# 38 instead of 73 dummy matmuls in TensorE's opening, ahead of the first MLP step

## Chip, cores and metric

The kernel runs on one core of a Trainium2 chip. The metric is the device time of one execution in microseconds (us). Engine names are those of the profile: PE is TensorE, PEld its weight loads, DVE VectorE, ACT ScalarE, POOL GpSimd, SP SyncE, which issues the loads and stores.

## What is computed

A linear-attention recurrence with a decay (4 batches, 8 heads, 768 steps, head dimension 48), whose output goes through a two-layer MLP with an ELU between (384 to 2048 to 384), all in fp32:

```python
for t in range(S):
    cur = np.einsum('bhd,bhe->bhde', u[None] * kt, vt)
    y[:, :, t] = np.einsum('bhd,bhde->bhe', rt, state + cur)
    state = wt[:, :, :, None] * state + np.einsum('bhd,bhe->bhde', kt, vt)
x = y as (B * S, H * D)
h = x @ w_in
g = np.where(h > 0.0, h, np.exp(np.minimum(h, 0.0)) - 1.0)
out = g @ w_out
```

The weights arrive in 64-bit form and are turned into fp32 on the chip.

## The kernel before

The 768 steps are cut into 6 chunks of 128, and each chunk into 4 units (24 in all). A unit's part of the recurrence is done in closed form. The four units of the first chunk go through these steps, which the text names by unit number and the trace by line:

- on DVE two scans of the decay (L436, L446), the product of r and k (L470) and the "hats", which multiply k and r by the scanned decay (L451)
- the *diagonal* on PE (`diag_pe`, L475, needs L470), copied by ACT (L479) and *spread* by ACT over a diagonal matrix (`spread_act`, L485, eight operations)
- the *scores* on PE (`score`, transposes L516 and products L528, needs the hats); ACT copies the transposes out (`trans_out`, L546)
- the *mask* on DVE (`mask`, L540, needs scores and spread)
- the *values* on PE (`value`, L503 and L568, needs mask and L546); ACT copies the result to x (`x_full`, L591)

The diagonal and the transposes share one PSUM bank (`single`, tag "pb"). The scores of units 0, 2 and 3 share two others (`pair`, tag "pa"); unit 1 borrows the accumulators of the MLP (`spare`).

The MLP works on one chunk (512 columns) at a time, in 16 slices of the hidden layer: `g1` (L259 for full fp32 weights, L263 for split ones), ELU on ACT and DVE (L267, L270, L273), `g2` (L291 or L294). In the first chunk six slices use fp32 weights and are done in halves, the first half needing units 0 and 1 alone. Meanwhile the weights are converted: a raw piece is loaded (`load_w`, L606), ACT and DVE work on it (L611, L616 or L618, L626, L630), and its buffer is then free for the next piece.

The order on every engine is fixed when the program is built: `Plan.order` lists all tasks by due times and model durations. Ahead of a task that stands in the table `FILL`, the emitting loop first puts that number of dummy matmuls:

```python
FILL = {("pd", 0): 29, ("s", 0): 12, ("v", 0): 1, ("pd", 1): 5, ("v", 1): 2, ("pd", 2): 7, ("s", 2): 5, ("g1", 0): 12}
...
    def warm(n):
        pw = spare()[2][:, 0:P]
        for _ in range(n):
            nc.tensor.matmul(pw, ones, ones, start=True, stop=True)
...
        for t in plan.order():
            warm(FILL.get(t["key"], 0))
            t["fn"]()
```

("pd", i) is the diagonal of unit i, ("s", i) its scores, ("v", i) its values and ("g1", 0) the first MLP product. A fill multiplies a 128x128 tile of ones by itself into an accumulator bank that the MLP clears later; nobody reads its result, and it waits for nothing but the ones. It stands in PE's queue, so what is behind it waits until it is done.

Of the kernel before, what the change touches and what calls it, by code (L numbers as in the profile page):

```python
# [41 lines left out]
LOW = ['DVE']*2+['ACT']*14  # L42
RAWS = ["raw0", "raw1", "x1a", "x1b"] * 2 + ["raw0", "raw1"] * 4
DUE = {0: 9.0}
FILL = {("pd", 0): 29, ("s", 0): 12, ("v", 0): 1, ("pd", 1): 5, ("v", 1): 2, ("pd", 2): 7, ("s", 2): 5, ("g1", 0): 12}


def _pieces():
    res = []
    for h in range(H):  # L50
        s, e = h * D, (h + 1) * D
        while s < e:
# [36 lines left out]
             g1={16: -3.5, 19: -3.5, 20: 4.25, 23: 5.75, 29: -7.5, 30: -8.25, 31: -13.25, 33: 21, 38: -15.75, 40: -29.75, 42: -33.75, 44: -17.5, 48: -70.75, 51: 26.75, 55: 44, 56: -10.5, 58: -10, 68: 34, 82: -8, 83: 12.5, 84: 6, 93: -7.5},  # L89
# [4 lines left out]
             s={4: -29.75, 9: -2.25, 12: -30.25, 13: 5, 21: 8.5},  # L94
             sp={4: -19.25, 5: 8.75, 9: 39.5, 13: 29.5, 17: -6.5},
             v={2: -5.5, 15: -2, 17: 6.75, 18: 24, 20: 22.25})
# [225 lines left out]
def rwkv_elu_kernel(ctx, tc, wkr, rk, vp, u, uz, gkrw, gv, gu, wraw, out):  # L322
# [84 lines left out]
# [4 lines that stand above are left out]
# [424 lines left out]
    with tc.manual_schedule():  # L835
# [3 lines that stand above are left out]
# [137 lines left out]
```

## Time and profile before

| | us |
|---|---|
| median of 3 runs | 518.42 (518.3 to 519.65) |
| the profiled execution | 517.97 |
| its span in the trace | 515.8 |
| PE busy in the span | 506.8 (98%) |
| PEld busy | 417.8 (81%) |
| DVE busy | 335.4 (65%) |
| ACT busy | 270.6 (52%) |
| mean granted clock | 0.997 |

The span is the stretch from the first to the last instruction of the program; the rest of the execution's time, 2.2 us, lies around it. Busy shares are means over stages with different limits. A matmul's duration in the trace overlaps the next one's, so the pace is read from one start to the next, not from durations.

### The profile page before, as it was taken

To read this page: it belongs to the slowest core of one execution; us is meant where nothing else is said; L and a number is where in the kernel's file an instruction comes from. 1 tells how busy PE (TensorE), PEld (TensorE's weight loads), DVE (VectorE), ACT (ScalarE), POOL (GpSimd) and SP (SyncE) were. 2 spreads that over 40 slices of the span, in tenths; PEclk is the share of its full clock that TensorE was granted. 3 is DMA by queue.
4 is the path that set the end of the run, shared out by engine and by line. 5 is a ranking of instruction groups with operands and counts; after the bars stand their busy time and mean duration, and the time that the engine had idled before them with its cause. 6 is when DMAs were issued, how large, how long until landed. Compare 5 with 4: busy or idle time off the path is not lost.

```text
span 515.8 us, 13882 instructions
## 1 busy us (share of the span) xinstructions
PE 506.8 (98%) x6070; PEld 417.8 (81%) x6070; DVE 335.4 (65%) x469; ACT 270.6 (52%) x520; POOL 97.1 (19%) x94
## 2 busy tenths in 40 slices
PE   9999999999999999999999999999999999999995
PEld 9998787787888888888788888887888877888884
DVE  6789999999589643498743487842499642423242
ACT  2779667657655344565545564443545443535351
POOL 2000123103455100264100174400161100000000
PEclk9999999999999999999999999999999999999998
DMA  8936944600843000856200674202332000010001
GB/s 258 337 132 201 319 139 142 189 3 4 260 117 106 3 3 3 243 154 160 57 19 3 197 204 143 75 0 79 99 101 56 22 1 3 0 62 0 1 1 66
DMA packets 18882, 51.09 MB, mean 99 GB/s; under 512 B 2304, under 2 KB 2688, under 8 KB 18816
## 3 DMA queue, kind: packets, MB, share of 16 engines
q1 hardware_dynamic: 18672, 50.08, 32.0%
q8 instruction: 49, 0.80, 0.6%
q14 instruction: 17, 0.14, 0.1%
q10 hardware_dynamic: 144, 0.07, 0.0%
HBM read 45.42 MB, written 4.72 MB: 97 GB/s over the span
## 4 chain that ended last, share of the span: by engine, by line
PE 86%; DVE 5%; ACT 3%; DMA 2%; issue 2%; POOL 0%; DVEq 0%; ACTq 0%; SPq 0%; POOLq 0%
PE ph L263 33%; PE acc L294 33%; PE pa L503 6%; PE acc L410 4%; PE pa L528 3%; PE pa L568 2%; PE ph L259 2%; PE acc L291 2%; PE pb L516 1%; DMA wx<-in_wkr_dram 1%; DMA wraw<-in_wraw_dram 1%; DVE m L273 1%; ACT m L270 1%; DVE wg L626 1%; ACT wg L611 1%
## 5 line engine op out<-in xcount | busy, mean ns | idle before, releaser
L273 DVE SCALAR_TENSOR_TENSOR m<-m,ph 128x512 f32<-128x512 f32 (+1 forms) x102 | 66.3, 651 | 98.3 <-ACT m L270 98.0
L267 ACT ACTIVATE m<-ph 128x512 f32<-128x512 f32 (+1 forms) x102 | 58.2, 571 | 108.7 <-PE ph L263 97.0
L263 PE MATMUL ph<-xh,w_l 128*128 128x512 f32 x270 | 105.4, 390 | 0.0
L294 PE MATMUL acc<-gh,w_l 128*128 128x512 f32 x268 | 104.6, 390 | 0.0
L281 DVE TENSOR_TENSOR gl<-m,gh 128x512 fp32r<-128x512 f32 x90 | 65.2, 726 | 39.4 <-ACT gh L277 39.3
L277 ACT CAST gh<-m 128x512 fp32r<-128x512 f32 x90 | 55.7, 619 | 59.4 <-PE acc L294 30.5
L294 PE MATMUL acc<-gh,w_h 128*128 128x512 f32 x180 | 71.9, 399 | 0.0
L263 PE MATMUL ph<-xh,w_h 128*128 128x512 f32 x180 | 71.6, 398 | 0.1
L294 PE MATMUL acc<-gl,w_h 128*128 128x512 f32 x180 | 70.3, 390 | 0.0
L263 PE MATMUL ph<-xl,w_h 128*128 128x512 f32 x180 | 70.1, 390 | 0.0
L270 ACT ACTIVATE m<-m 128x512 f32<-128x512 f32 (+1 forms) x102 | 61.9, 607 | 2.2
L263 PEld LDWEIGHTS ph<-xh,w_l 128*128 128x128 f32 x270 | 50.7, 188 | 10.9
L294 PEld LDWEIGHTS acc<-gh,w_l 128*128 128x128 f32 x268 | 50.3, 188 | 10.7
L458 POOL TENSOR_TENSOR rk<-rk 128x384 f32<-128x384 f32 x20 | 28.3, 1416 | 121.2 <-DMA rk<-in_rk_dram 116.7
L496 POOL TENSOR_SCALAR_AFFINE_SELECT am<-md 64x512 f32<-64x512 f32 x32 | 29.1, 910 | 113.5 <-DVE md L465 56.3
L263 PEld LDWEIGHTS ph<-xh,w_h 128*128 128x128 f32 x180 | 33.8, 188 | 7.8 <-DVE m L273 0.5
L294 PEld LDWEIGHTS acc<-gh,w_h 128*128 128x128 f32 x180 | 33.8, 188 | 7.7
L294 PEld LDWEIGHTS acc<-gl,w_h 128*128 128x128 f32 x180 | 33.8, 188 | 6.8 <-DVE gl L281 0.2
L263 PEld LDWEIGHTS ph<-xl,w_h 128*128 128x128 f32 x180 | 33.8, 188 | 6.7
L263 PE MATMUL ph<-xh,w_g 128*128 128x512 f32 x90 | 36.3, 403 | 0.1
L263 PE MATMUL ph<-xl,w_g 128*128 128x512 f32 x90 | 35.1, 390 | 0.0
L294 PE MATMUL acc<-gh,w_g 128*128 128x512 f32 x88 | 34.8, 396 | 0.0
(116 smaller groups left out, 754.2 us busy)
## 6 DMA issues: line engine op xcount, KB each, us to landing
wraw<-in_wraw_dram SPq DMA_DIRECT2D x16, 768.0 KB, 5.4
k<-in_wkr_dram SPq DMA_DIRECT2D x24, 448.0 KB, 6.7
rk<-in_rk_dram SPq DMA_DIRECT2D x20, 384.0 KB, 4.2
v<-in_vp_dram SPq DMA_DIRECT2D x24, 256.0 KB, 6.8
w<-in_wkr_dram SPq DMA_DIRECT2D x24, 227.9 KB, 4.4
out_dram<-o SPq DMA_DIRECT2D x17, 256.0 KB, 2.1
wx<-in_wkr_dram SPq DMA_DIRECT2D x8, 227.9 KB, 2.9
ub<-in_u_dram SPq DMA_DIRECT2D x1, 192.0 KB, 4.5
```

The source lines that it names most:

```text
L263: nc.tensor.matmul(ph, w[f][:, 0, k], y[:, k], start=(k == n == 0), stop=(k == NK - 1 and n == 2))
L267: act(s["m"], s["ph"], AF.Relu, scale=-1.0)
L270: act(s["m"], s["m"], AF.Exp, scale=-1.0)
L273: stt_(s["m"], s["m"], -1.0, s["ph"], ALU.add, ALU.max)
L277: nc.scalar.copy(s["gh"], s["m"])
L281: nc.vector.tensor_tensor(s["gl"], s["m"], s["gh"].bitcast(F32), ALU.subtract)
L294: nc.tensor.matmul(a_, w[f][:, 1, m], fold(s, g[:, a:b]), start=(first and n == 0), stop=(final and n == 2))
L410: nc.tensor.matmul(pw, ones, ones, start=True, stop=True)
L458: eng.tensor_tensor(u_["rk"][:, 0], u_["rk"][:, 0], u_["rk"][:, 1], ALU.mult)
L496: nc.gpsimd.affine_select(out=am[rs].rearrange("t q p s -> t (q p) s"), in_=u_["md"][rs].rearrange("t q p -> t (q p)").unsqueeze(2).broadc ...
L503: nc.tensor.matmul(u_["py"][32 * j:32 * j + 32, h, k], l, r, **flags)
L528: nc.tensor.matmul(pa[1 - q][ts, p], u_["k"][rs, p, ts], u_["r"][rs, p, ts], start=True, stop=True)
```

## The change

One table of numbers: fewer fills ahead of seven of the eight tasks.

```diff
-FILL = {("pd", 0): 29, ("s", 0): 12, ("v", 0): 1, ("pd", 1): 5, ("v", 1): 2, ("pd", 2): 7, ("s", 2): 5, ("g1", 0): 12}
+FILL = {("pd", 0): 15, ("s", 0): 6, ("v", 0): 1, ("pd", 1): 4, ("v", 1): 1, ("pd", 2): 3, ("s", 2): 2, ("g1", 0): 6}
```

The order on DVE, POOL and SP is the same as before. On ACT a few rows differ in the general path, which runs only if the decays are out of range and doesn't run with these inputs. On PE the start of the program now stands like this (L410 are the fills, L475 the diagonals, L516 and L528 the scores):

```order
 L970 UNCONDITIONAL_BRANCH
-L410 MATMUL acc<-ones 128x128 x29
+L410 MATMUL acc<-ones 128x128 x15
 L475 MATMUL pb<-ubd,rkc 128x2 x4
-L410 MATMUL acc<-ones 128x128 x12
+L410 MATMUL acc<-ones 128x128 x6
 L516 MATMUL pb<-ident,k 128x112 x4
 L528 MATMUL pa<-k 128x128 x8
-L410 MATMUL acc<-ones 128x128 x5
+L410 MATMUL acc<-ones 128x128 x4
 L475 MATMUL pb<-ubd,rkc 128x2 x4
```

Only counts differ; 14 fills fewer stand ahead of unit 0's diagonal, 6 ahead of its scores, 1 ahead of unit 1's diagonal. On PE around the first MLP product (L259) and unit 2's scores, behind unit 1's values (L568):

```order
 L568 MATMUL acc<-v,kt 64x48
 L568 MATMUL acc<-v,kt 48x48
-L410 MATMUL acc<-ones 128x128 x12
+L410 MATMUL acc<-ones 128x128 x6
 L259 MATMUL ph<-xf,w_f 128x256 x6
-L410 MATMUL acc<-ones 128x128 x5
+L410 MATMUL acc<-ones 128x128 x2
 L516 MATMUL pb<-ident,k 128x112 x4
 L528 MATMUL pa<-k 128x128 x8
```

Six fills fewer stand ahead of the first MLP product and three ahead of unit 2's scores. Between the two places, unit 2's diagonal has 4 fewer ahead of it and unit 1's values 1 fewer.

## Rows read from the trace of the kernel before

**Rows 1.** Busy time by stretch: length, each engine's busy us (instructions), granted clock, DMA.

```profile
40.00:60.00 20.00, 19.47 (x140) 15.89 (x140) 19.42 (x27) 17.74 (x36) 3.62 (x4) 1.00 0.80 254
101.00:200.00 99.00, 98.53 (x1635) 80.16 (x1636) 73.69 (x103) 53.02 (x97) 25.86 (x22) 1.00 0.22 65
```

**Rows 2.** Timeline of PE, 0 to 37 us: start us, length us, engine, line, operation.

```profile
1.07 9.63 PE L410 MATMUL acc<-ones 128*128 128x128 f32 x58 [1.07 <-POOL ones L377]
10.54 0.95 PE L475 MATMUL pb<-ubd,rkc 112*128 112x2 f32 x8
11.35 2.92 PE L410 MATMUL acc<-ones 128*128 128x128 f32 x24
14.11 0.55 PE L516 MATMUL pb<-ident,k 112*128 112x112 f32 x4
...
15.68 1.38 PE L410 MATMUL acc<-ones 128*128 128x128 f32 x10
16.90 0.95 PE L475 MATMUL pb<-ubd,rkc 112*128 112x2 f32 x8
17.71 0.47 PE L410 MATMUL acc<-ones 128*128 128x128 f32 x2
...
21.34 1.83 PE L410 MATMUL acc<-ones 128*128 128x128 f32 x14
23.01 0.95 PE L475 MATMUL pb<-ubd,rkc 112*128 112x2 f32 x8
...
26.05 2.94 PE L410 MATMUL acc<-ones 128*128 128x128 f32 x24
28.83 2.75 PE L259 MATMUL ph<-xf,w_f 128*128 128x256 f32 x12
31.42 1.28 PE L410 MATMUL acc<-ones 128*128 128x128 f32 x10
32.53 0.55 PE L516 MATMUL pb<-ident,k 112*128 112x112 f32 x4
...
36.39 0.86 PE L503 MATMUL pa<-am,v 128*32 128x128 f32 x24
```

**Rows 3.** Busy time in single microseconds: the first number in brackets counts PE's passes.

```profile
6.00:7.00 1.00, 1.00 (x7) 1.00 (x7) 1.00 (x3) 0.00 (x0) 0.00 (x0) 1.00 1.02 406
8.00:9.00 1.00, 1.00 (x12) 1.00 (x11) 1.00 (x2) 0.00 (x0) 0.00 (x0) 1.00 1.04 262
30.00:31.00 1.00, 1.00 (x7) 0.87 (x6) 0.74 (x1) 0.67 (x2) 0.00 (x0) 1.00 0.00 0
```

**Rows 4.** Timeline of DVE, 0 to 37 us; in square brackets idle time before, and releaser.

```profile
8.06 1.20 DVE L451 TENSOR_TENSOR k<-k,eg 112x1024 f32<-112x1024 f32 x1
...
15.90 1.35 DVE L540 COPY_PREDICATED am<-upper,pa 128x512 f32<-128x512 uint32 x2 [4.68 <-PE pa L528]
...
28.64 0.96 DVE L626 SCALAR_TENSOR_TENSOR w_f<-w_f,wraw 128x768 uint32<-128x768 uint32 x1 [0.91 <-ACT wraw L616]
29.52 1.22 DVE L451 TENSOR_TENSOR k<-k,eg 112x1024 f32<-112x1024 f32 x1
31.86 0.42 DVE L273 SCALAR_TENSOR_TENSOR m<-m,ph 128x256 f32<-128x256 f32 x1 [1.12 <-ACT m L270]
32.65 0.96 DVE L626 SCALAR_TENSOR_TENSOR w_f<-w_f,wraw 128x768 uint32<-128x768 uint32 x1 [0.37 <-ACT wraw L616]
...
35.00 1.33 DVE L540 COPY_PREDICATED am<-upper,pa 128x512 f32<-128x512 uint32 x2
```

**Rows 5.** Timeline of ACT, 0 to 37 us.

```profile
11.79 2.45 ACT L485 ACTIVATE am<-ident,md 128x128 f32<-128x128 f32 x8
...
14.93 0.51 ACT L546 COPY kt<-pb 128x448 f32<-128x448 f32 x1
...
26.55 0.46 ACT L591 COPY xf<-acc 128x384 f32<-128x384 f32 x1
```

**Rows 6.** The chain of work that ended last, 80 to 100 us, its longest piece.

```profile
86.74 6.19 DMA wraw<-in_wraw_dram
```

## Prediction

> **What bounds the kernel now.** I read the busy time by stage first, then TensorE's timeline of the first 37 us, then what VectorE and ScalarE wait for there. From 101 to 200 us TensorE is busy 98.53 of 99 us, VectorE 73.69 [rows 1]: nothing on PE is left to squeeze there, and work that begins earlier ends earlier. From 40 to 60 us PE is busy 19.47 of 20 us and VectorE 19.42 [rows 1]: both are full, so a gain of the opening reaches the end only if both engines get it.
>
> In the opening PE has no idle time after 1.07 us [rows 2]. It is full because fills stand between the real steps, and the question is whether a step starts when its inputs are ready or when the fill ahead of it is done. An fp32 fill matmul shows as two passes, so the 29 fills are the x58 at 1.07 us [rows 2]. The other engines answer the question: VectorE sits idle 4.68 us and then waits for PE's scores (L528), not PE for VectorE [rows 4]. Unit 0's hats end on VectorE at 8.06 + 1.20 = 9.26 us [rows 4], and its scores, which need them, begin on PE at 14.11 [rows 2]. The fills hold the real work back there.
>
> **What a fill costs.** The block of 24 passes at 26.05 lasts until 28.83, the one of 14 at 21.34 until 23.01 [rows 2]: 2.78 less 1.67 is 1.11 us for 10 passes, 0.112 us a pass. The first block is slower. If its last 28 passes took 0.112 each, its first 30 took 10.54 - 3.13 - 1.07 = 6.34 us, 0.211 each. The counts say the same: 7 passes touch the microsecond 6 to 7, 12 the one from 8 to 9 [rows 3]. So PE ran at its lower level (1.2 GHz) for some 6 us after its first matmul and at 2.4 GHz after that. The column PEclk shows 1.00 in both [rows 3]; I believe the pace of the passes.
>
> **The change, part by part.** It takes out 35 matmuls, 70 passes, all of them at 0.112 us if the clock rises where it does now: 28 passes ahead of unit 0's diagonal (3.13 us), 12 ahead of its scores (1.34), 2 ahead of unit 1's diagonal (0.22), 8 ahead of unit 2's diagonal (0.89), 2 ahead of unit 1's values (0.22), 12 ahead of the first MLP product (1.34), 6 ahead of unit 2's scores (0.67). Sum: 7.81 us. Each block is gained only as far as the step behind it has its inputs:
>
> - Unit 0's diagonal moves from 10.54 to 7.41. Its product (L470) is written before the second scan and the hats of 8.06 [rows 4], so it is ready by then. Gain 3.13.
> - Unit 0's scores move from 14.11 to 9.64. The hats end at 9.26. ScalarE's spread of unit 0 (11.79, 2.45 long) [rows 5] follows the diagonal and moves by 3.13, to 8.66 to 11.11. The mask (15.90 on VectorE) waits for scores and spread; the scores now end last, and the mask moves by 3.13 + 1.34 = 4.47, to 11.43. VectorE's idle time of 4.68 shrinks to 0.2.
> - Unit 1's diagonal would move to 12.21. It reuses unit 0's score bank, which ScalarE's copy (14.93, 0.51 long) [rows 5] must have left. That copy stands behind the spread and a weight conversion of some 0.8 us, so it now ends at about 12.3. PE waits 0.2 us.
> - The first MLP product moves from 28.83 by 6.95, to about 21.9. It needs unit 1's x (26.55 + 0.46 = 27.01) [rows 5], which hangs on unit 2's diagonal and moves by 3.13 + 1.34 + 0.22 - 0.2 + 0.89 = 5.4, to 21.6. It is just in time.
> - Unit 2's scores would move from 32.53 to 24.9. They need unit 2's hats on VectorE (29.52 + 1.22 = 30.74) [rows 4]. VectorE had moved by 4.46 at the first mask and gains the 0.91 it sat idle ahead of L626, since ScalarE is earlier too; so the hats end at 25.4 and PE waits 0.5.
> - Unit 2's values (36.39) need the mask at 35.00 on VectorE, 1.33 long. VectorE also loses the idle 1.12 and 0.37 [rows 4]: 4.46 + 0.91 + 1.12 + 0.37 = 6.86. The mask ends at 29.5, and PE waits 0.3 more.
>
> So PE gains 7.81 less waits of 0.2 + 0.5 + 0.3, that is 6.8, and VectorE gains 6.86 by its own idle time. Both engines carry the same 6.8 us into the full stage that follows, and I take **6.8**. What else could stand still is the loads. The first six pieces of raw weights leave in a full queue that runs dry by 30 us (0 GB/s from 30 to 31) [rows 3]. The fifth is converted on ScalarE between the spreads of units 2 and 3; if it has to wait for its landing it starts at most near 28, against 27 by the shift, and nothing before 33 us needs it. I cost that at nothing. From there each load is issued when a buffer comes free, so it moves along.
>
> The profiled execution took 517.97 us, 2.2 more than its span; less 6.8 that is 511.2. It lies 0.45 under the median of the runs (518.42), so my forecast for the median is **511.6 us**.
>
> Bounds of the sum: with no new wait at all it is 7.81 us, 510.6, or 510.1 on the profiled execution's level; with VectorE getting no more than its first 4.46, 514.0.
>
> **The rivals.**
>
> *The clock is lost (slower).* The fills also keep PE working, and the first 30 passes show what PE costs at the lower level: 0.211 against 0.112, 0.9 us more for each us of work. If with half the fills PE ran at 1.2 GHz from 7.41 until the first MLP product at 21.9, 14.5 us of work would take 13 us more: 524.6. It decides from 7.5 us of work at the lower level on, where 6.8 us is eaten up. Against it: PE's new idle time is 1 us in all. And from 16.90 to 21.34 the kernel before has just 2 passes of fill among diagonal, values and scores, yet the 14 passes that follow run at 0.112 [rows 2]: the level held through such a stretch, and the change makes more of them. Chance 0.09. The Trainium skill has a rule that speaks for this rival (TensorE: Matmul & The Clock Gate, section The HAM clock gate): the throttled state is the default, sustained matmul activity releases it and idleness brings it back. By that rule alone the thinner opening risks the 524.6; the trace agrees with it at the start, where the passes took 0.211, and shows no fall in the thin stretch.
>
> *The clock rises later.* The 30 passes that stay end at 7.41, and the rise comes shortly before that. In an execution where it comes only during unit 0's scores, the 3.9 us from 7.41 to 11.3 take up to 3.5 us more, and all that follows is late by as much: 511.6 to 515.1. For it: the fill now ends close to the rise. Against: PE goes straight on with diagonal, 12 passes and scores. Chance 0.11.
>
> *VectorE keeps its small waits.* If the idle 0.91, 1.12 and 0.37 stay, because ScalarE's chain of spread and conversion is no earlier than the first 4.46 us, VectorE brings just that into the full stage: 514.0. It was busy 19.42 of 20 us from 40 to 60 [rows 1], so it can't catch up. Against: ScalarE's operations there hang on PE steps that move by 5.4 and more. Chance 0.08. The Trainium skill (Perfetto Trace Analysis, section Identifying the Most-Contended Engine) warns that TensorE's matmul busy share is no measure of headroom and that weight-load time is. From 40 to 60 us weight loads are busy 15.89 of 20 [rows 1], so by that rule VectorE is the fuller engine and this case would be the one to bet on.
>
> *The gain is swallowed.* The chain of waits holds 6.19 us of waiting for a raw weight load from 86.74 on [rows 6]. If that load came at a fixed time, the opening would not matter: 518.4. Against: it is issued when a conversion frees its buffer, which moves too. Chance 0.05.
>
> **How the numbers follow.** Forecast 0.67; clock later 0.11, VectorE's waits 0.08, swallowed 0.05, clock lost 0.09. A measurement of this kernel tells about 0.3% (1.6 us) from no change; all of the first three lie beyond that on the fast side. So faster 0.86, same 0.05, slower 0.09. The range runs from 510.1 (no new wait) to 514.8, which takes in VectorE's case and most of the late clock.
>
> **What would show it.** In the new profile the first block of fills should end near 7.4 us and the first mask start near 11.4, with hardly any idle time before it; the first MLP product should start near 21.9, unit 2's mask near 28.2; PE's waits in the opening should sum to about 1 us; and every stage after 40 us should look as before, 6.8 us earlier. I am wrong if passes after 8 us take over 0.2 us, if VectorE still waits before L626 or L273 in the opening, or if the stage from 50 to 101 us gets longer.

## The result and the profile after

The changed kernel takes **512.17 us** (median of 4 runs, 511.97 to 512.88) against 518.36 for the kernel before beside it (4 runs, 517.35 to 519.65): a ratio of 0.9882 (the changed kernel's time over that of the kernel before), 95% interval 0.9858 to 0.9906. The forecast was 511.6. The execution profiled took 512.88 us, its span is 510.8.

TensorE's timeline of the opening in the changed kernel (start us, length us, engine, line, operation; in square brackets idle time before and its releaser):

```profile
1.07 5.55 PE L410 MATMUL acc<-ones 128*128 128x128 f32 x30 [1.07 <-POOL ones L377]
7.05 1.05 PE L475 MATMUL pb<-ubd,rkc 112*128 112x2 f32 x8 [0.43 <-DVE rkc L470]
7.97 1.59 PE L410 MATMUL acc<-ones 128*128 128x128 f32 x12
9.55 0.57 PE L516 MATMUL pb<-ident,k 112*128 112x112 f32 x4
...
12.14 1.02 PE L475 MATMUL pb<-ubd,rkc 112*128 112x2 f32 x8
...
21.68 2.76 PE L259 MATMUL ph<-xf,w_f 128*128 128x256 f32 x12
...
25.26 0.58 PE L516 MATMUL pb<-ident,k 112*128 112x112 f32 x4 [0.38 <-PE acc L410]
...
29.40 1.08 PE L503 MATMUL pa<-am,v 128*32 128x128 f32 x32 [0.19 <-DVE am L540]
```

Against [rows 2], unit 0's diagonal begins at 7.05 instead of 10.54, its scores at 9.55 instead of 14.11, the first MLP product at 21.68 instead of 28.83, unit 2's values at 29.40 instead of 36.39. PE now waits three times, 0.43, 0.38 and 0.19 us, 1.0 in all. The first block of fills ended some 0.8 us sooner than forecast, because the clock rose sooner (the same 30 passes lasted 5.55 us here and 6.45 in the run again below), and PE then waited for the product L470; the gain there stopped at what VectorE allows.

VectorE's timeline, same kernel:

```profile
8.06 1.20 DVE L451 TENSOR_TENSOR k<-k,eg 112x1024 f32<-112x1024 f32 x1
...
11.36 1.35 DVE L540 COPY_PREDICATED am<-upper,pa 128x512 f32<-128x512 uint32 x2 [0.16 <-PE pa L528]
...
23.07 0.95 DVE L626 SCALAR_TENSOR_TENSOR w_f<-w_f,wraw 128x768 uint32<-128x768 uint32 x1
...
25.08 0.41 DVE L273 SCALAR_TENSOR_TENSOR m<-m,ph 128x256 f32<-128x256 f32 x1
25.67 0.96 DVE L626 SCALAR_TENSOR_TENSOR w_f<-w_f,wraw 128x768 uint32<-128x768 uint32 x1 [0.18 <-ACT wraw L616]
...
28.01 1.33 DVE L540 COPY_PREDICATED am<-upper,pa 128x512 f32<-128x512 uint32 x2
```

The hats still begin at 8.06; the idle 4.68 before the first mask is 0.16, and the 0.91, 1.12 and 0.37 of [rows 4] are 0, 0 and 0.18. Unit 2's mask begins at 28.01 instead of 35.00. So VectorE carries 6.99 us into the full stage, PE as much (36.39 to 29.40). ScalarE shows the one load that stands still in the opening:

```profile
20.97 0.46 ACT L591 COPY xf<-acc 128x384 f32<-128x384 f32 x1
...
27.58 0.92 ACT L611 ACTIVATE w_f<-wraw 128x768 f32<-128x768 f32 x1 [0.66 <-DMA wraw<-in_wraw_dram]
```

It waits 0.66 for the fifth raw piece, and nobody waits for it. The stages behind the opening, by stretch (length, busy us of each engine, granted clock, DMA):

```profile
40.00:60.00 20.00, 18.30 (x114) 15.41 (x106) 18.25 (x24) 13.09 (x29) 2.66 (x2) 1.00 0.93 287
101.00:200.00 99.00, 99.00 (x1519) 80.38 (x1518) 71.23 (x98) 50.95 (x93) 25.23 (x22) 1.00 0.22 65
```

The steady stage is as full as in [rows 1]. The microseconds 40 to 60 now hold work that stood at 47 to 67. There 1.2 us of the gain go, as PE's timeline shows, first in the change, then in the kernel before:

```profile
49.66 1.56 PE L291 MATMUL acc<-m,w_f 128*128 128x256 f32 x6 [0.55 <-DVE m L273]
...
53.67 1.56 PE L259 MATMUL ph<-xf,w_f 128*128 128x256 f32 x6 [1.15 <-DVE m L273]
```

```profile
56.28 1.56 PE L291 MATMUL acc<-m,w_f 128*128 128x256 f32 x6 [0.19 <-DVE m L273]
...
59.48 1.56 PE L259 MATMUL ph<-xf,w_f 128*128 128x256 f32 x6 [0.34 <-DVE m L273]
```

PE waits for VectorE 0.36 us longer at the first place and 0.81 longer at the second: of the 6.99 us, 6.62 are left at the first (49.66 against 56.28) and 5.81 at the second (53.67 against 59.48). Behind the first loss stands a load. ScalarE's and VectorE's timelines in the change:

```profile
41.78 0.94 ACT L616 ACTIVATE wraw<-wraw 128x768 uint32<-128x768 uint32 x1 [0.68 <-DMA wraw<-in_wraw_dram]
```

```profile
43.84 0.56 DVE L588 TENSOR_TENSOR xl<-xf,xh 128x384 fp32r<-128x384 f32 x1 [0.47 <-ACT xh L584]
```

ScalarE waits for the ninth raw piece, and VectorE then for ScalarE; the kernel before has neither wait. The piece is issued 7.0 us earlier than before (35.9 against 42.9) but takes 5.8 us to land instead of 4.3. Behind the second loss stands a scan. VectorE's timeline, 50 to 60 us, and GpSimd's, 40 to 60 us:

```profile
51.26 2.04 DVE L436 TENSOR_TENSOR_SCAN eg<-w,reset 112x520 f32<-112x520 f32 x1
...
58.36 1.23 DVE L436 TENSOR_TENSOR_SCAN eg<-w,reset 112x520 f32<-112x520 f32 x1
```

```profile
50.96 1.25 POOL L458 TENSOR_TENSOR rk<-rk 128x384 f32<-128x384 f32 x1 [3.37 <-DMA rk<-in_rk_dram]
```

The same scan and product in the kernel before:

```profile
57.89 1.23 DVE L436 TENSOR_TENSOR_SCAN eg<-w,reset 112x520 f32<-112x520 f32 x1
```

```profile
58.36 1.54 POOL L458 TENSOR_TENSOR rk<-rk 128x384 f32<-128x384 f32 x1 [4.15 <-DMA rk<-in_rk_dram]
```

The scan of unit 5 starts 6.63 us earlier (51.26 against 57.89) and ends 5.82 earlier (53.30 against 59.12): it takes 2.04 instead of 1.23. Before, it began first and GpSimd's product was the stretched one (1.54; 1.00 us where nothing is beside it); now the product's data (unit 5's r and k) land in time for it to begin first. PE's second wait is for the operation right behind this scan (L273), so it loses the 0.81 us with VectorE. VectorE gets 0.42 of it back, since in the kernel before the subtraction L645 that follows is stretched in its turn (1.37 us; 0.95 in the change), but PE has lost its time by then.

What is left stays to the end. The chain of waits of the change, 80 to 110 us:

```profile
82.41 7.76 DMA wraw<-in_wraw_dram
...
94.86 0.65 DVE am L542
95.50 0.04 issue
95.55 1.17 PE pa L503 x71
```

It goes through another raw piece than the chain of [rows 6]. Two pieces are issued one after the other there; SyncE's timeline, first of the change, then of the kernel before:

```profile
80.93 1.81 SPq L606 DMA_DIRECT2D wraw<-in_wraw_dram  x2
```

```profile
86.74 1.81 SPq L606 DMA_DIRECT2D wraw<-in_wraw_dram  x2
```

Both are issued 5.81 us earlier and take about as long as before (6.2 and 7.8 us; 6.2 and 7.9 before), so these loads moved along. The values after them (101.47 before, 95.55 now) come 5.92 earlier. The last store is issued at 504.18 instead of 510.13, 5.95 earlier:

```profile
504.18 0.38 ACTq L309 DMA_DIRECT2D out_dram<-o  x1
```

From there to the end of the span are 6.6 us in this execution, 5.7 in that of before; the other three runs' spans are 509.9 to 510.3.

### The profile page after: what moved, and what is told of

Read it like the earlier page. It is cut to its first block, busy times and chain, and to the rows that moved or that the text cites. A ratio compares the mean times of both kernels' runs of the same rounds, so it can differ in the third digit from the quotient of the medians.

```text
span 510.8 us, 13742 instructions
## 1 busy us (share of the span) xinstructions
PE 498.9 (98%) x6000; PEld 409.6 (80%) x6000; DVE 336.5 (66%) x469; ACT 270.7 (53%) x520; POOL 94.8 (19%) x94
## 4 chain that ended last, share of the span: by engine, by line
PE 84%; DVE 5%; ACT 5%; DMA 3%; issue 1%; DVEq 0%; SPq 0%; ACTq 0%
PE acc L294 35%; PE ph L263 34%; PE pa L503 6%; DMA wraw<-in_wraw_dram 3%; PE pa L528 2%; PE pa L568 2%; PE pb L516 1%; PE ph L259 1%; ACT wraw L616 1%; PE acc L291 1%; DVE wg L626 1%; ACT m L270 1%; PE acc L410 1%; DVE m L273 1%; ACT m L267 1%
## 5 line engine op out<-in xcount | busy, mean ns | idle before, releaser
L273 DVE SCALAR_TENSOR_TENSOR m<-m,ph 128x512 f32<-128x512 f32 (+1 forms) x102 | 66.3, 651 | 96.6 <-ACT m L270 96.4
L458 POOL TENSOR_TENSOR rk<-rk 128x384 f32<-128x384 f32 x20 | 26.4, 1321 | 120.6 <-DMA rk<-in_rk_dram 120.2
```

The costliest lines, as they stand in the source:

```text
L273: stt_(s["m"], s["m"], -1.0, s["ph"], ALU.add, ALU.max)
L458: eng.tensor_tensor(u_["rk"][:, 0], u_["rk"][:, 0], u_["rk"][:, 1], ALU.mult)
```

## The experiments

My theory was that of the prediction: each block of fills is gained for itself, the gains add up, and both engines carry them on. Rivals: the fills' worth is the clock they hold; the gain of a part alone is lost on the way; and, once the profile after was seen, that the 0.8 us of the scan is a race between a load and VectorE. Each group of runs has runs of the kernel before beside it on the same chip ("before" in the brackets below); the chips differ from group to group.

### The two halves of the change

first15 takes out only the 14 fills ahead of unit 0's diagonal; rest_only takes out all the others and leaves that block. In the cuts here and below, a line with a plus alone stands in the place of the kernel's line `FILL`.

```diff
-FILL = {("pd", 0): 29, ("s", 0): 12, ("v", 0): 1, ("pd", 1): 5, ("v", 1): 2, ("pd", 2): 7, ("s", 2): 5, ("g1", 0): 12}
+FILL = {("pd", 0): 15, ("s", 0): 12, ("v", 0): 1, ("pd", 1): 5, ("v", 1): 2, ("pd", 2): 7, ("s", 2): 5, ("g1", 0): 12}
```

> Only the first block goes from 29 to 15 fills, all others as before. Theory (a fill is dead time up to the point where an input binds): unit 0's diagonal about 3.1 us earlier, VectorE's wait before the first mask 4.68 - 3.1 = 1.6 us, all behind moves by 3.1; end at 518.4 - 3.1 = 515.3 (514.8 to 515.8). Rival, gain comes from the later blocks alone: 518.4. Rival, gain is not additive because VectorE's later idle time is what counts: under 1 us.

```diff
+FILL = {("pd", 0): 29, ("s", 0): 6, ("v", 0): 1, ("pd", 1): 4, ("v", 1): 1, ("pd", 2): 3, ("s", 2): 2, ("g1", 0): 6}
```

> The first block stays at 29 fills, all others as in the change. Theory: VectorE gains 1.34 at the first mask and its idle 0.91 + 1.12 + 0.37 later, 3.7 in all; PE's 4.69 less waits of about 1 us gives the same; end at 518.4 - 3.7 = 514.7 (514.2 to 515.4). With the run that changes the first block alone this should add up to the change's gain, 6.2 to 6.8. Rival, only the first block matters: 518.4.

Measured: first15 517.07 (12 runs; before 517.46, 35 runs), ratio 1.0, 0.9972 to 1.0029; rest_only 515.25 (12 runs), 0.9956, 0.993 to 0.9981. Their openings do what the sum says: unit 2's mask begins at 31.67 and at 31.25, 3.33 and 3.75 earlier than before, together 7.08 where the whole change has 6.99. But by the last store (508.64 and 510.12 against 510.13) 1.49 and nothing is left. The execution of rest_only that was profiled took 518.3 us, 3 us more than the median of its runs; by medians 2.2 us of its gain arrive, and 515.25 lies within the times expected (which start from 518.4, not from 517.46), while first15 misses its 515.3. First the waits of VectorE, 36 to 110 us (waiting and releasing line: us in total, times, longest), of first15, then of rest_only:

```profile
DVE wg L626 <- ACT wg L611: 2.3, 1, 2.3
```

```profile
DVE wg L626 <- ACT wg L611: 2.1, 1, 2.1
```

This is behind a raw weight piece, the tenth, that took 6.2 us (first15) and 5.9 (rest_only) from issue to landing, where before, and in the change, it took 4.3 and 4.2. Second, collisions as in the change, here with the subtraction L645. VectorE's timeline in first15:

```profile
52.09 0.97 DVE L626 SCALAR_TENSOR_TENSOR wg<-wg,wraw 128x768 uint32<-128x768 uint32 x1 [2.31 <-ACT wg L611]
52.97 1.76 DVE L645 TENSOR_TENSOR w_l<-wg,w_h 128x768 fp32r<-128x768 f32 x1
...
58.19 1.75 DVE L645 TENSOR_TENSOR w_l<-wg,w_h 128x768 fp32r<-128x768 f32 x1
```

GpSimd's product began at 52.55 and at 58.13, just ahead of both. And in rest_only the clock falls behind PE's wait. PE's timeline, then the busy times by stretch (PE, PEld, DVE, ACT, POOL, then the granted clock):

```profile
54.42 2.77 PE L291 MATMUL acc<-m,w_f 128*128 128x256 f32 x6 [2.08 <-DVE m L273]
```

```profile
53.00:54.00 1.00, 0.00 (x0) 0.00 (x0) 1.00 (x2) 0.00 (x0) 0.22 (x1) 1.00 1.07 294
...
55.00:58.00 3.00, 3.00 (x9) 2.37 (x8) 3.00 (x5) 1.61 (x4) 0.58 (x1) 0.50 0.87 239
```

In first15 PE was idle from 53 to 55 us too, and the clock stayed at 1.00. The fall seems to come in some executions only: the three longest of rest_only's 12 runs, the profiled one among them, have a mean granted clock of 0.991 to 0.993, the other nine 0.996 to 0.998.

So an opening gain of 3.3 or 3.8 us isn't yet a gain of the kernel: in these two profiles most of it goes in the stage from 40 to 60 us, behind a load that lands late. "The gain is swallowed" is right for first15 and in part for rest_only, in a way I had not thought of. By medians the halves give 0.4 and 2.2 us, the whole 6: they don't add up. That the same load is behind it in the executions without a profile is not shown.

### Is the long raw piece the doing of the code's length?

In first15 a 16 KB packet of the instruction queue fell into the long piece. first15_pad has first15's fills and 14 tiny matmuls, so that PE's code is as long as before:

```diff
             warm(FILL.get(t["key"], 0))
+            for _ in range(14 * (t["key"] == ("pd", 0))):
+                nc.tensor.matmul(spare()[2][0:32, 0:32], ones[:, 0:32], ones[:, 0:32], start=True, stop=True)
             t["fn"]()
```

> As the run with 15 fills in the first block and all others as before, plus 14 dummy matmuls of 32 columns ahead of unit 0's diagonal, so that PE's code is as long as in the kernel before; they cost PE under 1.5 us. Theory (with the shorter code a 16 KB code fetch falls into the tenth raw weight piece, which then takes 6.2 us instead of 4.3): the piece takes about 4.3 us again, VectorE's wait of 2.3 us before L626 near 52 us is gone, end 2 to 3 us under the kernel before. Rival (that piece is slow for another reason, or at random): end as without the padding, level with the kernel before or up to 1 us above.

Measured: 517.29 (12 runs; before 518.55), ratio 0.9966, 0.9941 to 0.9991. The tenth piece took 4.6 us and VectorE waited 0.7 instead of 2.3 us. But the end stayed where it was (last store at 508.79, 1.34 earlier than before), since GpSimd's product now got ahead of L626 (1.73) and of a scan (2.04). The piece and its wait went as the code fetch would have it; the time didn't, and only_first and no_fill below, whose code is shorter still, show 4.2 us for that piece. Nor is such a packet enough to make a piece long: in all six profiles with the change's fills one follows the issue of the ninth piece within 0.6 us, and that piece took 4.2, 4.3, 4.4 and 4.5 us in four of them (swap_loads, late_load, again_b, again), 5.6 and 5.8 in two (swap_b, the change). **Not settled.**

### What the remaining fills are for

only_first keeps nothing but 15 fills ahead of unit 0's diagonal, no_fill nothing at all.

```diff
+FILL = {("pd", 0): 15}
```

> 15 fills ahead of unit 0's diagonal, none anywhere else. Theory (the remaining later fills stand in idle time): PE's waits take the place of the fills, the first mask at most 0.3 us earlier, end within 0.5 us of the change's 512.2. Rival (clock): with PE idle a third of the time from 7 to 25 us the clock falls, passes take 0.21 us again, 0.9 us for each us of work: 514 to 522.

```diff
+FILL = {}
```

> No fill at all, so PE's first work is unit 0's diagonal near 7.05 us. Rival (clock): PE begins at the lower level; if it rises during unit 0's scores, the first mask is 1 to 1.5 us later than with the change, 513.5; if it rises only with the first MLP product, 516 to 520. Theory that fills do nothing for the clock: 512.2, as with the change.

Measured: only_first 514.87, ratio 0.9939 (0.9911 to 0.9966); no_fill 514.75, 0.9929 (0.9901 to 0.9958); 12 runs each, before 517.46. Both beat the kernel before and neither reaches the change (0.9866 and 0.9872 in its two other measurements). For only_first the rival came true, not the theory; no_fill lies between the cases named. The busy times by stretch of only_first show why:

```profile
6.00:9.00 3.00, 2.00 (x17) 1.78 (x16) 3.00 (x4) 0.96 (x5) 0.00 (x0) 1.00 1.03 317
9.00:12.00 3.00, 2.58 (x20) 2.33 (x20) 2.17 (x4) 2.96 (x8) 0.00 (x0) 0.56 1.03 276
...
20.00:26.00 6.00, 5.78 (x61) 4.92 (x60) 5.78 (x8) 4.10 (x12) 0.00 (x0) 0.50 1.04 308
26.00:27.00 1.00, 1.00 (x5) 0.86 (x4) 0.79 (x2) 0.86 (x2) 0.00 (x0) 0.78 1.01 418
```

The clock had risen; PE then sat idle 1.41 us before unit 0's scores, the clock fell to the lower level (0.50 is 1.2 of 2.4 GHz), and it came back between 26 and 27 us. All 12 runs of only_first have a mean granted clock of 0.978 to 0.988, all 16 of the change one of 0.995 to 0.998. PE's timeline, only_first and then no_fill:

```profile
9.42 0.98 PE L516 MATMUL pb<-ident,k 112*128 112x112 f32 x4 [1.41 <-DVE reset L445]
...
12.34 1.87 PE L475 MATMUL pb<-ubd,rkc 112*128 112x2 f32 x8
...
24.93 3.59 PE L259 MATMUL ph<-xf,w_f 128*128 128x256 f32 x12 [0.22 <-ACT xf L591]
```

```profile
7.12 1.87 PE L475 MATMUL pb<-ubd,rkc 112*128 112x2 f32 x8 [7.12 <-DVE rkc L470]
...
25.58 3.54 PE L259 MATMUL ph<-xf,w_f 128*128 128x256 f32 x12 [0.21 <-ACT xf L591]
```

A diagonal of 0.95 takes 1.87 in both. The fills that the change leaves hold the clock, and that is worth 3.9 us at unit 2's mask (31.95 in only_first, 28.01 in the change) and 2.4 to 3.6 us at the end: the medians, from different chips, are 514.87 and 512.43 (the change in 12 runs), and against the kernel before beside each only_first gains 2.6 us, the change 6.0 and 6.2. The Trainium skill (TensorE: Matmul & The Clock Gate, section The HAM clock gate) has idleness bring the throttled state back; the trace agrees in only_first, where the clock fell behind 1.41 us of it, and shows that it need not: in first15 the clock stayed through 2.35 us.

### The first block longer instead of shorter

```diff
+FILL = {("pd", 0): 43, ("s", 0): 12, ("v", 0): 1, ("pd", 1): 5, ("v", 1): 2, ("pd", 2): 7, ("s", 2): 5, ("g1", 0): 12}
```

> The kernel before with 14 fills more in the first block, 43 in place of 29. Theory (dead time, 0.112 us a pass): unit 0's diagonal at 10.54 + 3.13 = 13.67, all behind it 3.1 us later, end 3.1 us over the kernel before (518.0 to 518.5 so far), that is near 521.3. Rival (the stage from 40 to 61 us takes up part of a shift of the opening, as it did when the first block alone was shortened): 0 to 2 us over it.

Measured: 520.59 (12 runs; before 518.72), ratio 1.0027, 1.0004 to 1.005: 1.9 us slower by medians, and at most 2.6. The diagonal of unit 0 begins at 13.24 instead of 10.54 and unit 2's mask at 37.70 instead of 35.00, both 2.70 later for 14 fills, not 3.1: the clock rose earlier in this execution than in that of before. It ends 3.62 later there (last store at 513.75; this execution took 1.4 us more than the median), with a scan of 2.03 us in the way. Between the two theories: a first block costs what it takes in the opening, and the stage after adds or takes away a microsecond.

### Which load lands first

again is the change once more; swap_loads has unit 5's r and k load issued after its load of w, so that GpSimd's product comes later.

> The change as it is, once more, beside the two runs below on one chip. Theory: the opening is 6.8 to 7 us earlier in every execution, and what scatters lies behind 50 us (raw weight loads of 4.2 or 6 us, a scan beside GpSimd); so about 6 us under the kernel before, with the scatter of the kernel before (some 4 us). Rival (clock): the clock falls in some executions because the fills are thin; then some runs lie 2 us and more above the rest and show a lower mean granted clock (under 0.994).

```diff
-        for t in plan.order():
+        tasks = plan.order()
+        place = {t["key"]: n for n, t in enumerate(tasks)}
+        one, two = place["ld_rk", 5], place["ld_w", 5]
+        tasks[one], tasks[two] = tasks[two], tasks[one]
+        for t in tasks:
```

> The change, with unit 5's r-and-k load issued after unit 5's decay load instead of before it. Theory (the 0.8 us lost near 51 us is GpSimd's product, started by that load, blocking VectorE's scan): the product starts later, the scan (L436) near 51.3 us takes 1.23 us instead of 2.04, PE behind it stays 6.6 us early instead of 5.8, end 0.8 us below the change. Rival (the loss comes from the loads' lengths): the scan's duration changes, the end does not.

Measured: again 512.58 (6 runs; before 518.55), ratio 0.9872, 0.9839 to 0.9905; swap_loads 510.97 (6 runs), 0.9848, 0.9815 to 0.9882. This time the change itself had no blocked scan (none stretched by the product). VectorE's and GpSimd's timelines in again:

```profile
50.89 1.23 DVE L436 TENSOR_TENSOR_SCAN eg<-w,reset 112x520 f32<-112x520 f32 x1
```

```profile
51.52 1.39 POOL L458 TENSOR_TENSOR rk<-rk 128x384 f32<-128x384 f32 x1 [4.31 <-DMA rk<-in_rk_dram]
```

The product began 0.63 after the scan, and the last store was issued at 503.36, 6.77 earlier than before. So the same program keeps or loses the 0.8 us from one execution to the next. I repeated both, and put the swap on the kernel before.

> The change a third time, as the measure for the two runs below. Opening as in its two profiles (first MLP product near 21.7 us, PE's idle time 1 us). Whether VectorE's scan near 51 us takes 1.23 or 2.04 us is open in one execution: theory says that it is 2.04 when unit 5's r-and-k load lands before the scan starts, 1.23 when it lands after. End 512 to 513.

> The exchanged loads a second time. Theory (GpSimd's product blocks the scan in some executions of the change and in none of this one): scan 1.23 us, PE at 61 us about 7 us earlier than in the kernel before, end 0.4 to 1.6 us under the change on the same chip. Rival (the first comparison was scatter): level with the change within 0.3 us.

> The kernel before, all 73 fills, with the same two loads exchanged. In its profile the scan started 0.5 us ahead of GpSimd's product and was not blocked, so theory expects little: 0 to 0.8 us under the kernel before, by the executions in which it is blocked. Rival (the exchange helps for another reason, such as an earlier decay load): 1 to 2 us under it, as in the change.

Measured (before 518.36, 17 runs): again_b 512.14 (6 runs), 0.9866 (0.9828 to 0.9904); swap_b 511.67 (6 runs), 0.9859 (0.9822 to 0.9896); before_swap 517.88 (12 runs), 1.0001 (0.9975 to 1.0028). In both again_b and swap_b the scan was blocked (2.04 us), in swap_b against what was expected; their last stores are at 505.27 and 504.40. PE's wait right behind the scan tells the two cases apart: 1.15 or 1.16 us in every profile in which the product began first (the change, again_b, swap_b, first43, first15_pad), 0.34 in before, again, swap_loads and late_load, in which the scan did. Swapping two neighbours doesn't decide the race, and without the change it is worth nothing. late_load therefore issues unit 5's r and k after its w and its k:

```diff
+        tasks = plan.order()
+        late = next(t for t in tasks if t["key"] == ("ld_rk", 5))
+        tasks.remove(late)
+        tasks.insert(next(n for n, t in enumerate(tasks) if t["key"] == ("ld_k", 5)) + 1, late)
+        for t in tasks:
```

> The change, with unit 5's r-and-k load issued after unit 5's decay load and its k load (the exchange put it after the decay load alone, and in its second profile the product still started 0.08 us ahead of the scan). Theory: the product can't start before 52.5 us, the scan near 51 us takes 1.23 us in every execution, PE at 61 us 6.8 to 7.3 us earlier than in the kernel before, end 511.0 to 511.5. Rival (the product then blocks the next operation of VectorE, a 0.95 us subtraction, by as much): scan 1.23, subtraction 1.7, end as with the change, 512 to 512.6.

Measured: 511.46 (6 runs, 510.51 to 512.69; before 518.72), ratio 0.985, 0.9818 to 0.9882. VectorE's and GpSimd's timelines:

```profile
51.12 1.22 DVE L436 TENSOR_TENSOR_SCAN eg<-w,reset 112x520 f32<-112x520 f32 x1
...
55.34 1.81 DVE L446 TENSOR_TENSOR_SCAN eg<-w,reset 112x520 f32<-112x520 f32 x1
```

```profile
54.13 1.92 POOL L458 TENSOR_TENSOR rk<-rk 128x384 f32<-128x384 f32 x1 [6.71 <-DMA rk<-in_rk_dram]
```

The first scan is free, the product now meets the second (1.81 instead of 1.24). The last store is issued at 502.55, 7.58 earlier than before. By medians the versions with the later load (511.46; 511.52 over swap_loads and swap_b) lie about 0.9 us under the change (512.43 over again and again_b). The intervals overlap, and late_load was measured beside other runs than the change; that it is better is likely, not shown.

## Why the prediction was right

| step | forecast | measured |
|---|---|---|
| unit 0's diagonal | 7.41 | 7.05 |
| unit 0's mask | 11.43 | 11.36 |
| first MLP product | 21.9 | 21.68 |
| unit 2's mask | 28.2 | 28.01 |
| PE's waits in the opening | 0.2 + 0.5 + 0.3 | 0.43 + 0.38 + 0.19 |
| gain carried into the full stage | 6.8 | 6.99; 6.77 and 6.86 in two other profiles |
| gain at the last store | 6.8 | 5.95; 6.77 and 4.86 in two other profiles |
| gain of the medians | 6.8 | 6.2; 5.9 over 86 runs of before and 12 of the change |

**What held.** The price of a fill, the caps by hats, x and mask, and VectorE's own idle time as a second count of the same gain all came out within 0.4 us. The two halves show the sum in the opening by itself: 3.33 and 3.75 for forecasts of 3.13 and 3.7. Only the first wait stood elsewhere: I had it at unit 1's diagonal, for the bank; it came at unit 0's, for L470. That the waits still sum to 1.0 is luck, as is the 0.2 us of gain beyond the forecast: both hang on a clock that rose early in this execution, and in again, where it rose later, PE waits 0.39 and 0.19 and carries 6.77 us. The lower end of the range, 510.1, is 510.16 by its own sum.

**What was mis-sized.** The step "Both engines carry the same 6.8 us into the full stage that follows", with "from there each load is issued when a buffer comes free, so it moves along". The loads are issued earlier, but they don't all land earlier by as much: the ninth raw piece took 1.5 us longer than before, and that cost 0.36 us (of the six profiles with the change's fills, only the two with a long ninth piece, the change and swap_b, have PE wait at that place). And in that stage GpSimd and VectorE hinder each other for 0.81 us whenever a product begins just ahead of a scan. The sum had both at nothing. One of the prediction's signs of being wrong came with them: the stage from 50 to 101 us got longer, by 0.7 us (PE is 6.62 us earlier at its start, 5.92 at its end). Behind it nothing more is lost in this profile.

The runs bear out the term of the scan in both directions. Right behind it PE is 7.00, 7.27 and 6.78 us earlier than before where the scan began first (again, swap_loads, late_load), and 5.81, 6.18 and 5.94 where the product did (the change, again_b, swap_b). At the last store the same six have 6.77, 6.44 and 7.58 against 5.95, 4.86 and 5.73, so it is one term of several: further on an execution loses up to 1.3 us or gains up to 0.8, which no run here separates.

**The rivals.** *The clock is lost* is real as a mechanism and wrong for this change: no stretch of it up to its last store shows a lower granted clock, while only_first shows one of 17 us. My price for it, 13 us, was far too high: only_first was 3.9 us behind the change at unit 2's mask, 2.4 to 3.6 at the end. I had doubled 14.5 us of PE's time, fills included; real steps that wait for other engines don't double (this is argued, no run separates it). *The clock rises later* costs little: unit 0's diagonal began at 6.97 to 7.46 in the six profiles with the change's fills, and in three of them PE waited for L470 first, so an early rise gains nothing. The kernel before pays in full: 10.54 in one profile, 9.12 in another with the same work before it (before_swap). So one thing the change buys is less dependence on when the clock rises. *VectorE keeps its small waits* was wrong, as the rows above show: 0.18 of the 2.40 us is left. *The gain is swallowed* was wrong for the change, whose load of [rows 6] is issued 5.81 us earlier, and right for one of its halves, first15.

## What to carry to other kernels

Dummy matmuls have two prices: those that end after the next step's inputs are ready delay it one for one, those that end before it cost nothing and hold the clock. So size each block by the time at which the other engines have the next step's inputs, read from their timelines, and where a block is taken away whole, look at the matmuls' lengths for the lower clock. And don't sum parts: where two engines are full behind the place of the gain, a part of 3 us can vanish there in a wait for a load, and a whole of 7 can arrive; measure the whole, with enough runs to see past a microsecond of chance.

## What the runs showed of the hardware

- The granted clock of the profile reads 1.00 until the first change is recorded: no_fill has 1.00 in every stretch up to 30 us, while its diagonal of 1.87 and its product of 3.54 us have the lengths that only_first has at 0.50. Durations tell, the column doesn't.
- The time at which the clock first rises scatters with the same work ahead of it: the same 58 passes of fill let unit 0's diagonal begin at 10.54, 10.38 and 9.12 us (before, rest_only, before_swap).
- A VectorE scan takes 2.04 instead of 1.23 us, and the subtraction L645 1.76 instead of 0.95, when GpSimd's product of two tensors began up to 0.4 us earlier; where the scan began first, the product took 1.54 instead of 1.00, and the subtraction behind the scan 1.37 (before). The Trainium skill (SBUF — State Buffer, section SBUF: two separate sides) has the two engines share a pair of ports as an exclusive lock, held by whoever starts first. The trace agrees: in the change the scan ended 1.09 us after the product (53.30 against 52.21), close to its own 1.23.
